# A Fourier filter and a SwiGLU layer on one core: filter read in four large calls, x calls first, dummy matmuls, and norms and stage A placed anew

## The chip, the cores and the metric

The kernel runs on one core of a Trainium2 chip. Five engines work side by side: TensorE (PE in the profile; PEld are its weight loads), VectorE (DVE), ScalarE (ACT), GpSimd (POOL) and SyncE (SP). Each runs its own instructions in the order in which they were issued, and engines wait for each other by semaphores. SP and POOL also issue the DMAs, each from a queue of its own. The metric is device time in microseconds; lower is better.

## What is computed

```python
def _attn_ref(x, filt_r, filt_i):        # x (8, 3008, 256); filters (1505, 256)
    X = np.fft.rfft(x, axis=1)
    Y = X * (filt_r + 1j * filt_i)[None, :, :]
    return np.fft.irfft(Y, n=x.shape[1], axis=1)

def _moe_ref(x, w_gate, w_val, w_out, rms_g):   # w_gate, w_val (256, 1536); w_out (1536, 256)
    xn = x / np.sqrt(np.mean(x * x, axis=-1, keepdims=True) + 1e-06) * rms_g
    g = xn @ w_gate
    return g * (1.0 / (1.0 + np.exp(-g))) * (xn @ w_val) @ w_out
```

The second takes the 24064 rows that the first gives. Everything is float32 outside; inside the matmul operands are float16.

## The kernel before

The transform over 3008 = 47 x 64 points is done as two short transforms, each a matmul with a constant table. For a batch b the stages are:

- A (`a_unit`, 12 units): x times `wa`, written to `t1` (two buffers), stored to DRAM by `z_store`, and read back transposed by `t2_load`. Batch 0 skips DRAM: `a0_unit` and transposes on TensorE (`tr0_unit`).
- B (`b_unit`, 16 units): `t2` times `wb` into a bank psb. Two products with the filter `ff` follow (`s_part` 0 and 1 on VectorE), their sum (`add_unit`, on GpSimd) and a transpose by DMA (`yt_load`). Batch 0 has `yt0_unit` in place of the last two: eight matmuls that add and transpose, and a copy on ScalarE. `b_soft` is the same unit with both products on GpSimd.
- back (`bi_unit`, 16 units): `yt` times `wi` into a bank psi, copied to `uu` by ScalarE, and transposed to `t4` by four DMAs (`t4_load`).
- norms (six a batch, m = 0 to 5): `n_unit` or, for the first two of batch 0, `n_first`; squares on ScalarE, the root on GpSimd (`stat_unit`, `rho`), the scaling on GpSimd (`xt_unit`), a DMA transpose to `xn` (`tr_unit`). Norms 0 and 1 of batch 0 use `q_unit`, `scale_split` and `scale_apply` on TensorE and VectorE.
- the layer: an item (b, m, jt) is one of 12 slices of the hidden width for 512 rows (384 in a few norms). `gv` makes pg and pv (four matmuls), ScalarE makes sg from pg, VectorE makes hh from pv and sg; `down`, two items later, adds four matmuls into po. There are 576 items.

TensorE's accumulator has few banks: psG and psV (pg, pv, two buffers each), psO (two), psM (one) and psB (one). Before the change psM serves `a_unit`, `bi_unit` and `n_unit` in turn, each holding it from its matmul to the end of its copy; psB serves `b_unit`.

The program has a start (lines 550 to 629), in which batch 0 goes through all stages up to its second norm, and a main loop over the items. Around each item a plan puts units of later batches. `at(slot, fn, ...)` enters a unit into the item numbered slot; `fit` moves it on until the bank ("M" is psM, "B" psB) is free in that slot and the estimated load of ScalarE ("A") or VectorE ("V") fits. What is planned first gets its slot first: norm 2 of batch 0, then for each further batch its stage A, its stage B with the back units, and its norms. Norms 3 to 5 of batch 0 are planned after stages A and B of batch 1.

In the start, lines 553 to 576 issue the loads. POOL's queue issues three chunks of x, the filter in calls over 24, 16, 7 and 24 partitions (`f_load`, 26 calls for four tiles, with the fourth x chunk among them), then the weights (`w_load`, 3 x 3 calls). A DMA from POOL's queue waits for the landing of the one eight places before it. The filter tiles are cleared first (`f_zero`), since some rows stay empty. `f_unit` transposes four rows of a tile on TensorE and copies a whole bank into `ff`; the rows of the second half of the frequencies are read in falling order by the DMA:

```python
            for a, e in ((0, 16), (16, 23)):
                nc.gpsimd.dma_start(t[p0 + H + a:p0 + H + e, lo:KC, :],
                                    raw(src, 64 * (a + 1) - c * KC - lo,
                                        [[64 * D, e - a], [-D, KC - lo], [1, D]]))
```

Lines 600 to 618 are a loop of twenty steps: step i does `b_unit` i, `yt0_unit` i - 2 and `bi_unit` i - 4, and in steps 1, 5 and 9 also four `f_unit`s, a `w_load` and a `w_gain` (weights times gain, on GpSimd). Lines 619 to 629 follow: `t4_first` (a transpose of the first four columns of `uu` on TensorE), `t4_load`, `n_first(0)`, `q_unit`, `scale_split`, `scale_apply`, the last `w_gain`, `n_first(1)`, and the x calls of batch 1.

Of the kernel before, what the change touches and what calls it, by code (L numbers as in the profile page):

```python
# [99 lines left out]
def kernel(  # L100
# [101 lines left out]
    def a_unit(b, i, eng="A"):  # L202
        c, r = divmod(i, XC // 2)
        if r == 0:
            st[b]["t1"][c] = t1p.tile([P, XC, D], FP16, tag="t1", name="t1")
        ps = bank(0, "psa")
        nc.tensor.matmul(ps, wa, st[b]["x"][c][:, 2 * r:2 * r + 2, :], start=True, stop=True)  # L207
        copy(eng, st[b]["t1"][c][:, 2 * r:2 * r + 2, :], ps.rearrange("p (a d) -> p a d", a=2))
# [36 lines left out]
    def b_soft(b, i):  # L245
        g, dh = divmod(i, 2)
        ps = bank(3, "psb")[:, 0:4 * KR]
        for k in range(4):
            kk = 4 * g + k
            nc.tensor.matmul(ps[:, ts(k, KR)], st[b]["t2"][kk // KC][:, kk % KC, ds(dh * P, P)],  # L250
                             wb[:, kk, :], start=True, stop=True)
        v = y_tile().rearrange("p a e -> p (a e)")[:, 0:4 * KR]
        nc.scalar.activation(out=v, in_=ps, func=AXT.Copy)
        s = [sp.tile([P, 4, KR], FP16, tag="s%d" % e, name="s%d" % e) for e in range(2)]
        v = v.rearrange("p (k r q) -> p k r q", k=4, r=2)
        st[b]["s"][i] = (v, s)
        s_part(b, i, 0, nc.gpsimd)
        s_part(b, i, 1, nc.gpsimd)
        add_unit(b, i)
# [13 lines left out]

    def bi_unit(b, i, eng="A", bk=0):
        g, dh = divmod(i, 2)
        yt = st[b]["yt"][g]
        ps = bank(bk, "psi")[:, 0:4 * KR].rearrange("p (k j) -> p k j", k=4)
        for k in range(4):
            nc.tensor.matmul(ps[:, k, :], yt[0:KR, k, dh, :], wi[:, 4 * g + k, :], start=True, stop=True)  # L279
        dst = uu[:, :, dh, 16 * g:16 * g + 16].rearrange("p c (k m) -> p c k m", k=4)  # L280
        copy(eng, dst, ps.rearrange("p k (c m) -> p c k m", c=H))
        if i == K2 // 2 - 1:
            half = uu[:, H - 1, :, :].rearrange("p e (k m) -> p e k m", k=K2)
            if b % 2:
                nc.gpsimd.tensor_copy(out=half[:, :, :, 2:4], in_=left)
            else:
                nc.gpsimd.tensor_copy(out=left, in_=half[:, :, :, 0:2])
# [67 lines left out]
    def tr0_unit(g, eng):  # L355
# [5 lines left out]
        if r == 0:  # L361
            t2_tile(0, c)
# [4 lines left out]
    def f_zero(c, eng):  # L367
        t = stg.tile([KR, KC, D], FP32, tag="stg", name="fs")
        if eng == "A":
            nc.scalar.activation(out=t.rearrange("p a d -> p (a d)"),  # L370
                                 in_=mhalf[0:KR, 0:1].to_broadcast([KR, KC * D]), func=AXT.Copy, scale=0.0)
        else:
            nc.vector.memset(t, 0.0)
        fst[c] = t

    def f_load(c):
        t = fst[c]
        lo = 1 if c == 0 else 0
        for src, p0 in ((filt_i, 0), (filt_r, SL)):
            nc.gpsimd.dma_start(t[p0:p0 + H, :, :].rearrange("p a d -> p (a d)"),  # L380
                                raw(src, c * KC, [[64 * D, H], [1, KC * D]]))
            for a, e in ((0, 16), (16, 23)):
                nc.gpsimd.dma_start(t[p0 + H + a:p0 + H + e, lo:KC, :],
                                    raw(src, 64 * (a + 1) - c * KC - lo,
                                        [[64 * D, e - a], [-D, KC - lo], [1, D]]))
            if c == 0:
                nc.gpsimd.dma_start(t[p0 + H:p0 + SL, 0, :], raw(src, 32, [[64 * D, H], [1, D]]))

    def f_unit(c, j, eng, bk):
        half, dh = divmod(j, 2)  # L390
        ps = bank(bk, "psf")[:, 0:4 * KR].rearrange("p (a q) -> p a q", a=4)
        for a in range(4):
            nc.tensor.transpose(ps[:, a, :], fst[c][:, 4 * half + a, ds(dh * P, P)], idf)  # L393
        k0 = KC * c + 4 * half
        copy(eng, ff[:, dh, k0:k0 + 4, SL:3 * SL], ps)

    def f_neg(c):
        k = slice(KC * c, KC * c + KC)
        nc.gpsimd.tensor_scalar(out=ff[:, :, k, 0:SL], in0=ff[:, :, k, SL:2 * SL], scalar1=-1.0,
                                scalar2=1.0, op0=ALU.mult, op1=ALU.mult)  # L400

    def yt0_unit(i, eng, bk):
# [6 lines left out]
        if dh == 0:  # L409
            yt_tile(0, g)  # L410
        copy(eng, st[0]["yt"][g][0:KR, :, dh, :], ps)

    def t4_first():
# [5 lines left out]
        for q, eng in ((0, "A"), (2, "V")):  # L419
# [3 lines left out]
    def n_first(m):  # L423
        y = y_tile()
        sq = xtp.tile([P, 4, D], FP16, tag="xt", name="sq").rearrange("p (a e) d -> p a (e d)", a=2)
        for dh in range(2):
            ps = bank(1 + dh if m == 0 else 0, "psn")
            for q in range(4):
                n1p = 4 * m + q
                src = st[0]["t4f"][:, q] if m == 0 else st[0]["t4"][n1p // XC][:, n1p % XC]  # L430
                nc.tensor.matmul(ps[:, ts(q, P)], src[:, ds(dh * P, P)], wai, start=True, stop=True)
            nc.scalar.activation(out=sq[:, dh, :], in_=ps, func=AXT.Square)
            if m == 0:
                nc.vector.tensor_scalar(out=y[:, dh, :], in0=ps, scalar1=1.0, scalar2=None,
                                        op0=ALU.mult)
            else:
                nc.scalar.activation(out=y[:, dh, :], in_=ps, func=AXT.Copy)
# [3 lines left out]
    def q_unit(m):  # L441
        sq = st[0]["sq"].pop(m)
        ps = psB.tile([P, 4], FP32, tag="mb", name="psq")
        for q in range(4):
            for dh in range(2):
                nc.tensor.matmul(ps[:, q:q + 1], sq[:, dh, ts(q, P)], ones,
# [15 lines left out]
    def scale_apply(m, bk):  # L462
# [8 lines left out]
        for dh in range(2):  # L471
            nc.vector.tensor_tensor(out=xn[:, :, dh, :], in0=ps.rearrange("p (q t) -> p q t", q=4),
                                    in1=y[:, dh, :].rearrange("p (q t) -> p q t", q=4), op=ALU.mult)
# [57 lines left out]
    def w_load(q):  # L531
# [4 lines left out]
        wst[q] = t  # L536
        nc.gpsimd.dma_start(wo[:, ts(q, JT // 3), :],
# [11 lines left out]
    with tc.manual_schedule():  # L549
# [3 lines left out]
        for c in range(3):  # L553
            x_load(0, c)
# [10 lines left out]
        f_zero(0, "V")  # L565
        f_zero(1, "A")
        f_zero(2, "V")
        f_zero(3, "A")
        nc.vector.memset(ones, 1.0)
        f_load(0)  # L570
        x_load(0, 3)
        f_load(1)
        f_load(2)

        E = ("A", "V")
        for dh in range(2):
            a0_unit(0, dh, E[dh], 1 + dh)
        for g in range(4):
            wi_group(g, E[g % 2])
        for gq in (1, 2):  # L580
            for dh in range(2):
                a0_unit(gq, dh, E[dh], 1 + dh)
        for g in range(4, 8):
            wi_group(g, E[g % 2])
        for dh in range(2):
            a0_unit(3, dh, E[dh], 1 + dh)
        for j in range(4):
            f_unit(0, j, E[j % 2], 1 + j % 2)
        f_neg(0)
        f_load(3)  # L590
        for i in range(3):
            for t in ss3[i:i + 1]:
                nc.gpsimd.memset(t, 0.0)
        for gq in (4, 5):
            for dh in range(2):
                a0_unit(gq, dh, E[dh], 1 + dh)
        tr0_unit(0, "V")
        tr0_unit(1, "A")
        UN = K2 // 2
        for i in range(UN + 4):  # L600
            if i < UN:
                b_unit(0, i, (0, 3)[i % 2])
                s_part(0, i, 1)
            if i < 3:
                for g in (2 * i + 2, 2 * i + 3):
                    tr0_unit(g, E[g % 2])
            if i >= 2 and i - 2 < UN:
                yt0_unit(i - 2, "A", 1)
            if i >= 4:
                bi_unit(0, i - 4, "A", 2)  # L610
            if i % 4 == 1 and i // 4 + 1 < NC:
                c = i // 4 + 1
                for j in range(4):
                    f_unit(c, j, E[j % 2], 1 + j % 2)
                f_neg(c)
                w_load(c - 1)
                if c > 1:
                    w_gain(c - 2)
        t4_first()
        for c in range(NXC):  # L620
            t4_load(0, c)
        n_first(0)
        q_unit(0)
        scale_split(0)
        scale_apply(0, 1)
        w_gain(2)
        n_first(1)
        for c in range(NXC):
            x_load(1, c)
# [17 lines left out]
        def fit(slot, *need):  # L647
# [13 lines left out]
            for r, d, cost in need:  # L661
                load[r][slot + d] += cost
# [11 lines left out]
        def a_plan(b, slots, engs):  # L674
            for i in range(12):
                e = engs[i % len(engs)]
                s = fit(slots[i], ("M", 0, 1), (e, 0, 0.6))
                at(s, a_unit, b, i, e)
# [25 lines left out]
        at(1, q_unit, 1)  # L704
        at(3, scale_split, 1)
        at(5, scale_apply, 1, 3)
        norm_plan(0, 2, (12, 14), (2, 3, 6))
        for b in range(1, B):
            t = (b - 1) * 72
            if b == 1:  # L710
                z = a_plan(b, [i for i in range(12)], "AV")
                b_at, lags = [z + 7 + (5 * i + 2) // 3 for i in range(16)], (7, 7)
                soft = range(1, 16, 3)
            elif b == 2:
                z = a_plan(b, [46 + i for i in range(12)], "V")
                b_at, lags, soft = [z + 7 + 5 * i // 2 for i in range(16)], (8, 9), ()
            else:
                at_ = [t - 87 + 4 * i for i in range(12)]
                z = a_plan(b, [s - (s % JT == 1) for s in at_], "V")
# [3 lines left out]
            if b == 1:  # L723
                for m in range(3, 6):
                    norm_plan(0, m, (12 * m - 14, 12 * m - 12), (2, 3, 6))
# [52 lines left out]
```

## Time and profile before

Three runs took 919.36, 917.9 and 919.18 us, with a median of 919.18. The profiled execution took 918.45 us, of which its span, from the first instruction to the last, is 916.7.

| stretch, us | what runs | PE busy | DVE | ACT | POOL | PE clock | DMA GB/s |
|---|---|---|---|---|---|---|---|
| 0 to 20 | tables, x, stage A of batch 0 | 7.04 | 8.58 | 9.34 | 10.64 | see text | 167 |
| 20 to 51 | filter, stages B and back of batch 0 | 29.53 | 23.08 | 23.11 | 24.86 | see text | 193 |
| 51 to 60 | first norm | 4.00 | 3.70 | 3.01 | 4.76 | 0.61 | 167 |
| 60 to 76 | first items | 13.20 | 5.91 | 6.35 | 3.61 | 0.68 | 155 |
| 76 to 160 | items with batch 1 beside them | 81.50 | 55.43 | 55.74 | 38.37 | 1.00 | 120 |
| 160 to 176 | items 59 to 66 | 10.95 | 7.78 | 6.27 | 4.18 | 0.89 | 201 |
| 176 to 916 | the rest | 724.32 | 496.79 | 482.51 | 225.61 | 1.00 | 109 |

Busy times are in us within the stretch. The clock is the share of full speed that TensorE was granted. Up to 29 us the page gives 1.00, but the matmuls show half: eight of L350 take 1.05 us at 17.8 us, and sixteen transposes of L359 take 1.88 us at 27.4 us against 1.06 at 32.0.

How to read the lines. A wait reads "engine, group, <-, who ended the wait: us in total, times, longest us". A line of the timeline reads "start, us, engine, line, operation, written <- read, shape, times", and in brackets the idle time before it and what ended it. Matmuls are pipelined and their ends are modelled, so the distance from one start to the next is the surer measure: two matmuls of 512 columns start 0.22 us apart at full clock.

### The profile page before, as it was taken

The numbers are of one execution on the slowest core, as the hardware profiler recorded it, in microseconds if no ns is written. First come the engines' busy times: TensorE is split into PE (matmuls) and PEld (weight loads), VectorE is DVE, ScalarE is ACT, GpSimd is POOL, SyncE is SP. The second block draws the span as 40 slices with busy tenths as digits, with TensorE's granted clock in tenths as the row PEclk, the third lists the DMA queues.
The fourth block names the chain that finished last, engine by engine and source line by source line (L and its number), as shares of the span: only waits on it lengthen the run. The fifth ranks groups of instructions, "written<-read, shape, count | busy, mean of one in ns | idle before, by whom it ended". The sixth has DMA issues, their size and how long they took to land.

```text
span 916.7 us, 17045 instructions
## 1 busy us (share of the span) xinstructions
PE 870.5 (95%) x6151; PEld 538.3 (59%) x6151; DVE 601.3 (66%) x988; ACT 586.3 (64%) x1264; POOL 312.0 (34%) x362
## 2 busy tenths in 40 slices
PE   4969999799999999999999999999999999999997
PEld 3935555455565556655665566665566666665554
DVE  4836666577767776776767776677666666555554
ACT  4745676467557665677567675677657775677543
POOL 5841572245314441344304442244304441122100
PEclk9969999999999999999999999999999999999999
DMA  9897655896776456665584747543365332431101
GB/s 163 184 195 143 149 88 102 188 186 138 138 145 117 97 116 141 111 146 126 102 178 102 111 104 151 118 122 93 97 131 121 70 70 79 93 75 47 58 24 47
DMA packets 199429, 106.94 MB, mean 117 GB/s; under 512 B 160106, under 2 KB 184168, under 8 KB 199152
## 3 DMA queue, kind: packets, MB, share of 16 engines
q1 hardware_dynamic: 190800, 86.25, 42.2%
q0 software_dynamic: 8544, 19.60, 13.0%
q8 instruction: 48, 0.79, 0.4%
q14 instruction: 37, 0.30, 0.1%
HBM read 44.74 MB, written 35.65 MB: 88 GB/s over the span
## 4 chain that ended last, share of the span: by engine, by line
PE 75%; DVE 9%; ACT 6%; DMA 4%; issue 3%; POOL 2%; SPq 0%; ACTq 0%; DVEq 0%; POOLq 0%
PE po L503 22%; PE pg L486 22%; PE pv L486 20%; DVE hh L491 4%; ACT sg L490 4%; DVE t L198 3%; PE psi L279 3%; PE psb L239 2%; PE psn L307 2%; PE psa L207 2%; DMA wb<-wb_t 1%; DMA xn<-xt 1%; DMA yt<-ss 1%; ACT junk L315 1%; PE psf L393 1%
## 5 line engine op out<-in xcount | busy, mean ns | idle before, releaser
L491 DVE TENSOR_TENSOR hh<-pv,sg 128x512 f16<-128x512 f32 (+1 forms) x576 | 391.6, 680 | 283.7 <-ACT sg L490 192.5
L490 ACT ACTIVATE sg<-pg 128x512 f16<-128x512 f32 (+1 forms) x576 | 337.5, 586 | 265.6 <-PE pg L486 261.2
L503 PE MATMUL po<-wo,hh 128*128 128x256 f16 x2256 | 343.1, 273 | 1.1 <-DVE o L509 0.7
L486 PE MATMUL pg<-xn,wg 128*128 128x512 f16 (+1 forms) x1152 | 339.5, 376 | 4.8 <-DMA xn<-xt 4.8
L486 PE MATMUL pv<-xn,wv 128*128 128x512 f16 (+1 forms) x1152 | 339.4, 376 | 0.0
L503 PEld LDWEIGHTS <-hh 128*128 128x128 f16 x2256 | 212.2, 98 | 119.1 <-issue 11.5
L264 POOL TENSOR_TENSOR ss<-s,s 128x384 f16<-128x384 f16 x112 | 101.8, 910 | 284.5 <-DVE s L232 253.5
L486 PEld LDWEIGHTS <-wv 128*128 128x128 f16 x1152 | 113.3, 98 | 132.1 <-issue 2.3
L486 PEld LDWEIGHTS <-wg 128*128 128x128 f16 x1152 | 112.7, 98 | 19.2 <-issue 6.0
L333 POOL TENSOR_TENSOR xt<-y,rho 128x1024 f16<-128x1024 f32 (+1 forms) x46 | 85.3, 1854 | 2.9
L315 ACT ACTIVATE junk<-y 128x256 f16<-128x256 f32 x180 | 74.2, 412 | 2.8
L196 ACT ACTIVATE uu<-psi 128x384 f16<-128x384 f32 x128 | 62.2, 487 | 12.9 <-PE psi L279 12.4
L229 DVE TENSOR_TENSOR s<-psb,ff 128x384 f16<-128x384 f32 x123 | 67.3, 547 | 2.8 <-PE psb L239 2.6
L232 DVE TENSOR_TENSOR s<-psb,ff 128x384 f16<-128x384 f32 x123 | 67.2, 547 | 0.0
L196 ACT ACTIVATE y<-psn 128x512 f32<-128x512 f32 x92 | 54.1, 588 | 8.7 <-PE psn L307 4.8
L279 PEld LDWEIGHTS <-yt 96*128 96x128 f16 x512 | 35.2, 97 | 40.1 <-issue 14.8
L198 DVE CAST t<-psa 128x512 f16<-128x512 f32 x78 | 53.0, 680 | 0.0
L279 PE MATMUL psi<-wi,yt 96*128 96x96 f16 x512 | 42.8, 205 | 8.9 <-DVE t L198 5.9
L323 POOL TENSOR_SCALAR u<-ss 128x4 f32<-128x4 f32 (+1 forms) x46 | 8.9, 193 | 114.4 <-ACT junk L315 114.0
L325 POOL TENSOR_TENSOR rho<-u,mhalf 128x4 f32<-128x4 f32 (+1 forms) x46 | 46.5, 1010 | 3.8
L239 PE MATMUL psb<-wb,t 96*128 96x96 f16 x492 | 41.4, 207 | 0.3
L239 PEld LDWEIGHTS <-t 96*128 96x128 f16 x492 | 29.4, 98 | 15.1 <-issue 4.7
(82 smaller groups left out, 386.4 us busy)
## 6 DMA issues: line engine op xcount, KB each, us to landing
out_dram<-o SPq DMA_DIRECT2D x40, 512.0 KB, 3.5
xc<-in_x_dram POOLq DMA_DIRECT2D x31, 384.0 KB, 5.8
z_tmp<-t SPq DMA_DIRECT2D x28, 384.0 KB, 4.8
t<-z_tmp SPq DMA_DIRECT2D x28, 384.0 KB, 5.6
out_dram<-o SPq DMA_DIRECT2D x8, 384.0 KB, 3.2
ws<-in_moe_w_gate_dram POOLq DMA_DIRECT2D x3, 512.0 KB, 5.5
ws<-in_moe_w_val_dram POOLq DMA_DIRECT2D x3, 512.0 KB, 6.2
yt<-ss SPq DMA_TRANSPOSE x56, 3.2
```

Of the source, the lines that this page charges most:

```text
L196: nc.scalar.activation(out=out, in_=in_, func=AXT.Copy, **({} if scale is None else {"scale": scale}))
L198: nc.vector.tensor_copy(out=out, in_=in_)
L229: eng.tensor_tensor(out=o, in0=ps, in1=f1, op=ALU.mult)
L239: nc.tensor.matmul(ps[:, ts(k, KR)], st[b]["t2"][kk // KC][:, kk % KC, ds(dh * P, P)], wb[:, kk, :], start=True, stop=True)
L264: nc.gpsimd.tensor_tensor(out=ss3[g % 3][:, :, dh, 0:KR], in0=s[0], in1=s[1], op=ALU.add)
L279: nc.tensor.matmul(ps[:, k, :], yt[0:KR, k, dh, :], wi[:, 4 * g + k, :], start=True, stop=True)
L315: nc.scalar.activation(out=junk, in_=y[:, i, ts(u, D)], func=AXT.Square, accum_out=ss[:, 2 * i + u:2 * i + u + 1])
L333: nc.gpsimd.tensor_tensor(out=xt[:, 0:n, :], in0=y.rearrange("p a (u d) -> p (a u) d", u=2)[:, 0:n, :], in1=rho[:, 0:n].unsqueeze(2).to_br ...
L486: nc.tensor.matmul(ps[:, 0:w], wt[:, dt_, ts(jt, P)], xn[:, 0:nq(b, m), dt_, :], start=(dt_ == 0), stop=(dt_ == 1))
L490: nc.scalar.activation(out=sg[:, 0:w], in_=pg[:, 0:w], func=AXT.Silu)
L491: nc.vector.tensor_tensor(out=hh[:, 0:w], in0=pv[:, 0:w], in1=sg[:, 0:w], op=ALU.mult)
L503: nc.tensor.matmul(po[s4 // 2][:, s4 % 2, :], hh[:, ts(s4, P)], wo[:, jt, :], start=(jt == 0 and s4 % 2 == 0), stop=(jt == JT - 1 and (s4 ...
```

## The change

The start. All four x chunks of batch 0 are issued first. `f_load` makes one call for 94 rows of a filter and half of its columns (four calls in all, 770 KB each, and two calls of one row); nothing has to be cleared but one column of `ff`. `f_unit` transposes four rows of 94 and writes each bank in two copies, one by VectorE and one by ScalarE, with the falling order in the copy's access pattern. All `tr0_unit`s and the `f_unit`s of the first half stand ahead of the twenty-step loop, and the groups are taken in the order 0, 4, 1, 2, 3, 5, 6, 7. Two units (steps 4 and 5) are done by `b_soft` and a DMA transpose. The weights' calls come earlier; `w_gain` and the x calls of batch 1 stand after the second soft unit. The first norm's halves are split by rows instead of by columns. `fill(n)` issues n matmuls of 512 columns on zeros, whose result nobody reads. `n_first(1)` moves into item 2.

The plan. Norms 2 to 5 of batch 0 are planned first, at items 10, 20, 31 and 42. A unit of stage A may take psM or psB and ScalarE or VectorE, whichever fits earliest; with VectorE it keeps its bank for two items.

```diff
-    def a_unit(b, i, eng="A"):
+    def a_unit(b, i, eng="A", bk=0):
...
-        ps = bank(0, "psa")
+        ps = bank(bk, "psa")
...
+    def f_load(f, half):
+        t = stg.tile([P, KC, D], FP32, tag="stg", name="fs")
+        src = (filt_i, filt_r)[f]
+        if half == 0:
+            nc.gpsimd.dma_start(t[0:94].rearrange("p (h a) d -> p h (a d)", h=2),
+                                raw(src, 0, [[16 * D, 94], [12 * D, 2], [1, 4 * D]]))
+            nc.gpsimd.dma_start(t[94:95, 0, :], raw(src, NF - 1, [[D, 1], [1, D]]))
         else:
+            nc.gpsimd.dma_start(t[0:94].rearrange("p a d -> p (a d)"),
+                                raw(src, 4, [[16 * D, 94], [1, KC * D]]))
+        fst[(f, half)] = t
...
+    def f_unit(f, half, j, bk):
+        h, dh = divmod(j, 2)
+        r0 = (12 * h, 4 + 4 * h)[half]
...
+            nc.tensor.transpose(ps[:, a, 0:n], t[0:n, 4 * h + a, ds(dh * P, P)], idf[0:n, 0:n])
+        v = ps.rearrange("p a (q s) -> p s a q", s=4)
...
+        e = ("A", "V") if j % 2 else ("V", "A")
+        copy(e[0], fk[:, :, r0:r0 + 4, o:o + H], v[:, 0:2])
+        hi = slice(o + H, o + 2 * H - 1)
+        if r0:
+            copy(e[1], fk[:, ::-1, 13 - r0:17 - r0, hi][:, :, ::-1, :], v[:, 2:4, :, 0:H - 1])
...
+    def fill(n):
+        ps = psO.tile([P, 512], FP32, tag="po1", name="pf")
+        for _ in range(n):
+            nc.tensor.matmul(ps, wa, ss3[0].rearrange("p k e q -> p (k e q)")[:, 0:512], start=True, stop=True)
...
-        for c in range(3):
+        for c in range(NXC):
             x_load(0, c)
...
+        a0(3, 4, 5)
+        fill(4)
+        for f in range(2):
+            for j in range(4):
+                tr0_unit(ORD[4 * f + j], E[j % 2])
+                f_unit(f, 0, j, 1 + j % 2)
...
+                if p in soft:
...
+                    b_soft(0, unit(p), v)
+                    if p == soft[1]:
+                        yt_load(0, ORD[p // 2])
+                        w_gain(0)
+                        for c in range(NXC):
+                            x_load(1, c)
+                        w_gain(1)
+                        w_gain(2)
...
         t4_first()
+        fill(2)
...
         n_first(0)
+        fill(4)
         q_unit(0)
         scale_split(0)
+        fill(7)
         scale_apply(0, 1)
-        w_gain(2)
-        n_first(1)
-        for c in range(NXC):
-            x_load(1, c)
+        fill(5)
...
+                opts = []
+                for k in "MB":
+                    opts.append((k, "A", ((k, 0, 1), ("A", 0, 0.6))))
+                    opts.append((k, "V", ((k, 0, 1), (k, 1, 1), ("V", 0, 0.68))))
+                k, e, need = min(opts, key=lambda o: fit(slots[i], *o[2], keep=False))
+                s = fit(slots[i], *need)
+                at(s, a_unit, b, i, e, 0 if k == 'M' else 3)
...
-        norm_plan(0, 2, (12, 14), (2, 3, 6))
+        for m, n_at in ((2, 10), (3, 20), (4, 31), (5, 42)):
+            norm_plan(0, m, (n_at, n_at + 2), (2, 3, 6))
...
-            if b == 1:
-                for m in range(3, 6):
-                    norm_plan(0, m, (12 * m - 14, 12 * m - 12), (2, 3, 6))
```

## The prediction

> **What bounds the kernel now.** I read the page first, for the busy shares:
>
> ```profile
> span 916.7 us, 17045 instructions
> PE 870.5 (95%) x6151; PEld 538.3 (59%) x6151; DVE 601.3 (66%) x988; ACT 586.3 (64%) x1264; POOL 312.0 (34%) x362
> PEclk9969999999999999999999999999999999999999
> ```
>
> TensorE sets the time, so time can be won only where it is idle, slow, or held between two matmuls. The third line shows where it is slow: the third slice (46 to 69 us). Second, the waits of TensorE from 60 us on:
>
> ```profile
> PE psi L279 <- DVE t L198: 5.9, 22, 0.6
> PE pg L486 <- DMA xn<-xt: 4.8, 2, 4.5
> PE psa L207 <- DMA xc<-in_x_dram: 2.5, 1, 2.5
> PE psa L207 <- DVE t L198: 1.8, 4, 0.8
> PE psn L307 <- DVE t L198: 0.9, 3, 0.5
> ```
>
> Third, the timeline of TensorE around the two long waits and around one of the many short ones:
>
> ```profile
> 60.23 1.06 PE L486 MATMUL pg<-xn,wg 128*128 128x512 f16 x2
> 61.09 1.06 PE L486 MATMUL pv<-xn,wv 128*128 128x512 f16 x2
> 64.61 0.59 PE L207 MATMUL psa<-xc,wa 128*128 128x512 f16 x1 [2.46 <-DMA xc<-in_x_dram]
> ...
> 160.72 0.60 PE L503 MATMUL po<-wo,hh 128*128 128x256 f16 x4
> 165.81 0.80 PE L486 MATMUL pg<-xn,wg 128*128 128x384 f16 x2 [4.48 <-DMA xn<-xt]
> ...
> 393.01 0.49 PE L486 MATMUL pv<-xn,wv 128*128 128x384 f16 x2
> 394.08 0.33 PE L279 MATMUL psi<-wi,yt 96*128 96x96 f16 x4 [0.59 <-DVE t L198]
> ```
>
> The first block: the loop starts at 60.23 with matmuls of 0.43 us start to start instead of 0.22, and then stands until x of batch 1 lands. The second: item 60 (batch 0, norm 5) has no `xn` for 4.5 us, and its first matmuls run slowly again. The third: psi starts 1.07 us after pv, where two matmuls of that width need 0.33. Its bank psM was filled by `a_unit` one item earlier and VectorE empties it late, because its queue holds hh first.
>
> **The change, part by part.** Times are set against the profiled execution: 918.45 us, of which 916.7 is span; the median of the runs is 0.7 us higher.
>
> *Start, up to the first b_unit (27.10 now).* POOL's queue shows its loads going out as earlier ones land: the waits on x end at 6.47, 8.93 and 11.70 us, so an x chunk takes 2.5 to 2.8 us, and the fourth, now issued at 13.84 behind eight filter calls, is then in by 14.3. a0 for groups 3 to 5 can follow the last wi group at once (17.8 us, about 2.7 us at the slow clock, as 0.86 to 1.05 us each now), and four dummies at 0.43 us end at 22.4. Then comes a stage that the kernel did not have: all eight `tr0_unit` and eight `f_unit` before the first b_unit. ScalarE carries four casts of 1.02 us, eight copies of some 190 elements (rows: 490 ns for 384, 597 for 512, so about 0.33 each) and about 0.7 us of small copies: 7.4 us. The two copies of one bank run one after the other on two engines, which I put at another 1.1. The first b_unit starts near 30.9, 3.8 later than now.
>
> In return the twenty-step loop that follows, which VectorE paces (s_part to s_part 0.47 us, two a unit, 0.93 a step), loses three transposes' casts (2.0 us), swaps six filter copies of 0.55 for eight of 0.36 (0.4), and two units (four s_parts, 1.9) go to POOL: 4.3 us. POOL takes 1.0 + 1.0 + 0.91 us for each, so 5.8 us after the fifth unit's bank is read, and then the transpose's 3.2 us to landing; bi of these units comes eight steps later, 7.4 us. That is 1.6 us short: a wait of 1.5 (0 if the queue slips, 4 if the transfer lands like the slowest ones). The clearing of the filter tiles (two memsets of 1.77 on VectorE, 3.7 us on ScalarE) goes away at no gain, since both engines wait for x at 6.9 us. So far: +3.8 - 4.3 + 1.5 = +1.0.
>
> *Landing of the filter.* Now the eight units of the first half need 1.54 MB, where the first four needed 0.77 (in at 19.98). The trace has no load over 94 partitions. Bounds: at the 410 GB/s of the best stretch (38 to 40 us, wide weight loads) both calls are in by 18.1 and nothing waits. At the 143 GB/s of the filter stage (25 to 30 us), they are in by 14.3 + 10.8 = 25.1 when served in order, +2.7 after 22.4; if all four calls share that rate side by side, by 35.9, +13.5. I take the middle, +2.7, since it is the same tensor on the same queue and the filter loads land there in the order of issue; I keep 0 and +13.5.
>
> The Trainium skill speaks against this part (DMA: Bandwidth & Descriptors, "Why a DMA increments its semaphore by 16 and not by 1"): a transfer is split over the largest number up to 16 that divides its outer dimension, so 94 rows would use two of the 16 engines, where 24 rows use twelve. With that page's 27 GiB/s an engine, 770 KB would take an estimated 13.3 us, in by 27.6, which would make this term +5.2 and the forecast 2.5 us later. The page names an exception for loads from this queue, and no row here shows which holds.
>
> *From the last bi to the first item (50.76 to 60.23).* The chain of waits runs through transposes, t4f, psn, sq, y, u, rho, hl, psr, xn. Its operations stay; the eight psn matmuls of norm 1 (two times about 0.43) leave, psr and psn run at full clock (psr 0.93 to about 0.5), and xn no longer precedes a slow queue: -1.3. The fills (2, 4, 7, 5 of 0.22) lie inside waits of 0.9 to 1.9 us; if that cover went, the longest would cost 1.5. POOL now does three w_gain (2.7 us each) and four x calls (2.5 us) before rho, some 16 us after the first soft unit with its sums; by my times it ends about 1 us before rho is due. At the early end that is free, at the late end +2.
>
> *Items 0 to 12.* From 60.23 to the 14th pg at 87.50 are 27.3 us; thirteen items of 1.30, twelve psa of 0.22 and 0.7 of the first norms make 20.2. So 7.1 are lost to the x wait, the slow clock and psM. x now goes out some 13 us before the loop. New: `n_first(1)` stands inside item 2 with one bank for both halves; its second half waits for sg, sq and y on ScalarE, 1.3 us, and down(0) is queued behind it. Also `z_store` of chunk 0 leaves in item 5 and `a_unit` 6 wants its buffer in item 7: two items of about 1.6 us against 5.4 to landing; the copy waits on ScalarE, sg is queued behind it, and so again for chunk 1. Part is absorbed by two banks of pg: 2.5 us, with 0 and 4 as ends. With 0.4 for the rest: -7.1 + 1.3 + 2.5 + 0.4 = -2.9.
>
> *Item 60.* Norms 3 to 5 of batch 0 go ahead of batch 1; the transpose for item 60 leaves in slot 50 instead of 57. That takes away 4.66 us idle and about 1.7 from the slow clock that followed (165.8 to 169.1). What is late next: batch 1's first transpose now leaves in slot 69 for item 72, three items or 4.2 us ahead, where transposes land in 2.8 to 10.5 us, 3.5 at the median. I put 1.5 (0 to 4). -6.4 + 1.5 = -4.9.
>
> *Stage A elsewhere.* By start-to-start times, 44 places from 176 us on have a VectorE cast of stage A in psM followed in the next item by another user of psM; together they lose 14.6 us (0.33 each). The waits count 8.6, because a modelled matmul's end covers part. After the change such a unit is on ScalarE, or in psB, or keeps its bank for two items. ScalarE copies already in psM followed in the next item (n_unit after bi_unit, 41 places) lose 0.0. ScalarE gains about 55 copies of 0.6 us, 33 us at 65% busy; I give back 2. -12.6.
>
> Sum: 1.0 + 2.7 - 1.3 - 2.9 - 4.9 - 12.6 = -18.0: 900.5 in the profiled execution's terms, 901 as a median.
>
> **The rivals.** (a) The filter calls share their rate side by side: +13.5 instead of +2.7, 912. For it: in the filter stage packets of many calls are under way together. Against it: calls landed in order. (b) ScalarE takes the place of VectorE: its extra copies delay sg, and of the 12.6 us only 3 remain, 910. For it: it is 64% busy on average, and slots such as 50 to 60 hold eight copies. Against: 217 us of its idle time after 200 us is waiting for pg. (c) The fills do not hold the clock, and the change doesn't do that part of what it says: the first items lose another 4 us, 905. (d) Slower: a call over 94 rows lands at the speed of one call now, 192 KB in 7.4 us, or 26 GB/s; 770 KB then take 29.6 us, and the two calls of the first half one after the other end at 73.5. tr0 and f_unit start 51 us late: 949. This decides as soon as the first-half calls land after 22.4 + 2.7 + 18.0 = 43 us; side by side at that speed (43.9) it would just be even.
>
> **How the numbers follow.** The forecast has 0.60 (its own range 892 to 907), (a) 0.15, (b) 0.13, (c) 0.05, (d) 0.07. Low end: no filter wait, no wait for soft units or buffers, and nothing given back on ScalarE take off 10.7: 890. High end: (a), 912. About 0.2% (1.8 us) is what these runs can tell from no change. Faster 0.92, same 0.02, slower 0.06.
>
> **What would show it.** Right: first pg near 62 with matmuls 0.22 apart, no wait of pg for xn around item 60, no psi waiting for DVE t, and f_unit waiting for the filter until about 25 us. Wrong: f_unit starting after 35 us (a, d); sg's waits for pg shrinking while psi or psn wait for ScalarE (b); PEclk low in the third slice (c); or a wait of pg for xn at item 72 over 4 us.

## The result, and the profile after

Twenty runs of the changed kernel have a median of 925.51 us (919.1 to 929.03), twenty of the kernel before 919.11 (916.17 to 920.62). The ratio is 1.0061, with an interval of 1.0045 to 1.0078: slower by about 0.6%, where the forecast was 2% faster. The profiled execution of the changed kernel took 919.34 us, the third fastest of its twenty, so the two profiles lie only 0.9 us apart, and the medians 6.4.

From the page of the changed kernel:

```profile
span 917.6 us, 17059 instructions
PE 864.5 (94%) x6157; PEld 538.9 (59%) x6157; DVE 567.5 (62%) x946; ACT 612.9 (67%) x1326; POOL 305.8 (33%) x345
PEclk9689999989999999999999999999999999999999
```

TensorE has less to do than before (864.5 us instead of 870.5) and still ends later, so it waits more. Its waits over the whole span that bear on the argument (what waits, for whom; us in total, times, longest). Left out are 6.3 us for the first x chunk, 6.2 before, and 3.0 for the table `wb`, 5.6 before:

```profile
PE psf L391 <- DMA fs<-in_filt_i_dram: 15.9, 1, 15.9
PE psa L207 <- DVE t L198: 4.9, 1, 4.9
PE psi L283 <- ACT yt L196: 2.8, 4, 0.7
PE psn L312 <- ACT t L196: 1.8, 1, 1.8
PE pg L499 <- DMA xn<-xt: 1.0, 1, 1.0
```

Of the waits shown before, psi for VectorE's `t` (5.9 us, 22 times) is gone, and pg for xn is down from 4.8 to 1.0 us. Two large ones are new: 15.9 us for the filter and 4.9 us for a tile of stage A. The timeline of TensorE shows the first (start, busy, line, and in brackets the idle time before and its releaser):

```profile
17.57 0.71 PE L364 MATMUL pst<-ident,uu 128*96 128x128 f16 x8
34.17 0.86 PE L391 MATMUL psf<-idf,fs 95*128 95x95 f32 x4 [15.90 <-DMA fs<-in_filt_i_dram]
```

The start times of pg split the span. In us, from the traces of the profiled executions, those of the experiments beside them:

| kernel | up to item 0 | items 0 to 13 | 13 to 62 | 62 to 74 | 74 to the end | span |
|---|---|---|---|---|---|---|
| before | 60.2 | 27.3 | 82.5 | 17.2 | 729.5 | 916.7 |
| after | 77.9 | 23.2 | 76.7 | 23.8 | 716.0 | 917.6 |
| e1_flat_rows | 63.0 | 22.9 | 76.6 | 25.2 | 716.2 | 903.9 |
| e2_eighty_rows | 61.8 | 23.1 | 78.2 | 26.1 | 716.0 | 905.2 |
| e4_batch3_later | 65.4 | 23.2 | 78.2 | 30.2 | 717.0 | 914.0 |
| e6_stageA_alone | 60.8 | 25.4 | 88.7 | 19.0 | 715.5 | 909.4 |
| e7_x3_later | 64.9 | 22.9 | 75.6 | 25.6 | 722.1 | 911.1 |
| e8_A2_spread | 60.6 | 22.7 | 76.9 | 20.6 | 715.7 | 896.5 |
| e9_x3_spaced | 62.8 | 22.5 | 74.8 | 20.0 | 721.6 | 901.7 |
| e10_spread_no_fills | 62.3 | 24.9 | 76.3 | 19.6 | 715.4 | 898.5 |

The changed kernel loses 17.7 us before the first item and 6.6 between items 62 and 74, and wins 4.1, 5.8 and 13.5 elsewhere: +0.9. The experiments take these one by one. Their times are medians; a ratio compares them with runs of the kernel before on the same chip. One execution of e5, at a lower clock than its others, is in the slower state and is left out of its numbers.

A row of the table is one execution, and not always a typical one. Those of e1 and e8 were the fastest of their runs, those of e4, e6 and e7 the slowest, 2.5 to 4.5 us from their medians; a difference of that size between two rows can be the execution's.

### The profile page after: what moved, and what is told of

It is laid out like the page before. It is cut to its first block, busy times and chain, and to the rows that moved or that the text cites. A ratio compares the mean times of both kernels' runs of the same rounds, so it can differ in the third digit from the quotient of the medians.

```text
span 917.6 us, 17059 instructions
## 1 busy us (share of the span) xinstructions
PE 864.5 (94%) x6157; PEld 538.9 (59%) x6157; DVE 567.5 (62%) x946; ACT 612.9 (67%) x1326; POOL 305.8 (33%) x345
## 4 chain that ended last, share of the span: by engine, by line
PE 83%; DMA 7%; DVE 4%; ACT 3%; issue 2%; POOL 1%; SPq 0%; ACTq 0%; DVEq 0%; POOLq 0%
PE po L516 25%; PE pg L499 24%; PE pv L499 24%; DMA fs<-in_filt_i_dram 3%; DMA z_tmp<-t 2%; PE psi L283 2%; PE psb L239 2%; PE psn L312 2%; PE psa L207 2%; ACT sg L503 1%; DVE hh L504 1%; DVE o L522 1%; DMA xn<-xt 1%; PE psy L416 1%; DMA t<-z_tmp 1%
## 5 line engine op out<-in xcount | busy, mean ns | idle before, releaser
L266 POOL TENSOR_TENSOR ss<-s,s 128x384 f16<-128x384 f16 x114 | 103.7, 910 | 267.7 <-DVE s L232 246.3
L229 DVE TENSOR_TENSOR s<-psb,ff 128x384 f16<-128x384 f32 x121 | 66.2, 547 | 5.7 <-PE psb L239 3.9
L232 DVE TENSOR_TENSOR s<-psb,ff 128x384 f16<-128x384 f32 x121 | 66.2, 547 | 0.0
L196 ACT ACTIVATE t<-psa 128x512 f16<-128x512 f32 x61 | 35.9, 596 | 6.3 <-DMA z_tmp<-t 2.4
## 6 DMA issues: line engine op xcount, KB each, us to landing
fs<-in_filt_i_dram POOLq DMA_DIRECT2D x2, 752.0 KB, 29.4
```

Source lines behind the costliest of these rows:

```text
L196: nc.scalar.activation(out=out, in_=in_, func=AXT.Copy, **({} if scale is None else {"scale": scale}))
L229: eng.tensor_tensor(out=o, in0=ps, in1=f1, op=ALU.mult)
L232: eng.tensor_tensor(out=o, in0=ps[:, :, ::-1, :], in1=f2, op=ALU.mult)
L266: nc.gpsimd.tensor_tensor(out=ss3[g % 3][:, :, dh, 0:KR], in0=s[0], in1=s[1], op=ALU.add)
```

## The experiments

### Where the 15.9 us for the filter come from

The DMA view of the changed kernel over 0 to 45 us gives, in 40 equal slices, the busy share of the 16 engines in tenths and the rate, then an issue with its median time to landing:

```profile
DMA  0197999999999999999933222222222310000079
GB/s 0 33 70 134 201 221 244 243 248 242 236 232 79 193 187 227 222 204 157 149 69 98 95 102 106 102 106 106 98 85 106 131 80 36 0 0 0 4 138 419
fs<-in_filt_i_dram POOLq DMA_DIRECT2D x2, 752.0 KB, 29.4
```

From 23 to 33 us only two to three tenths of the engines are busy, and the rate is 100 GB/s. The packets tell which call this is: all are pieces of 4 KB, those of the first half, on 4.1 engines, 25 GB/s each; the 8 KB pieces of the second half, issued later, had run on some 12 engines before. Of the 16 increments by which the first call reports its landing, 14 came at 15 to 16 us and the last two at 33.1 and 33.7 us: two engines carried it. Of the two calls of the second half, twelve increments each had come by 22.1 and 25.7 us, and the last four at 35.5 to 38.6: on four engines they stood behind the first half's rows. e1 writes the same bytes in two dimensions instead of three:

```diff
-            nc.gpsimd.dma_start(t[0:94].rearrange("p (h a) d -> p h (a d)", h=2),
-                                raw(src, 0, [[16 * D, 94], [12 * D, 2], [1, 4 * D]]))
+            for h in range(2):
+                nc.gpsimd.dma_start(t[0:94, 4 * h:4 * h + 4].rearrange("p a d -> p (a d)"),
+                                    raw(src, 12 * h, [[16 * D, 94], [1, 4 * D]]))
```

> Edit: the changed kernel, but each first-half filter call (94 rows x two pieces of 4 KB, three dimensions) is written as two calls of 94 rows x one piece of 4 KB (two dimensions, as the second-half calls have). Same bytes, same pieces, same queue, two calls more. Theory A (few engines: a call of the three-dimensional form is given to 2 of the 16 DMA engines, at about 25.7 GB/s each, which the trace of the changed kernel shows as 103 GB/s on 4 engines from 25 to 33 us): the first half is spread over 16 engines and lands at 20 to 23 us, the first f_unit starts by 24 us instead of 34.2, the first pg at 65 to 68 us instead of 77.9, and the run takes 905 to 911 us. The spread of the changed kernel's runs (919 to 929 us) should shrink to that of the kernel before (4 us) if it comes from this landing. Rival B (the calls share one rate, whatever their form): f_unit still starts at 33 to 35 us, and the time stays at 919 to 929 us. Rival C (the landing moves but the loop behind it is held by something else, such as the soft units' transposes): f_unit by 24 us, first pg not before 72 us, 913 us or more.

910.13 us (905.62 to 913.31), ratio 0.9907, interval 0.9886 to 0.9927: 15.4 us below the changed kernel's median, at the upper end of what theory A gave. The same view of e1, and a line of its timeline:

```profile
DMA  0187999999999999999996002999990006999999
fs<-in_filt_i_dram POOLq DMA_DIRECT2D x2, 376.0 KB, 12.1
```

```profile
20.54 0.50 PE L392 MATMUL psf<-idf,fs 95*128 95x95 f32 x4
```

All engines are busy until the filter is in, its first half lands in 12 to 13 us, and f_unit starts at 20.5 us with no idle time before it. B and C are out: the calls share no fixed rate, since the bytes moved at 240 to 280 GB/s in e1 and at 100 in the changed kernel while twelve engines stood idle, and the first pg moved by 14.9 us, with the landing. What did not shrink as expected is the spread of the runs (7.7 us). e2 keeps the three dimensions and changes the number of rows alone:

```diff
+            for lo, n in ((0, 80), (80, 14)):
+                nc.gpsimd.dma_start(t[lo:lo + n].rearrange("p (h a) d -> p h (a d)", h=2),
+                                    raw(src, 16 * lo, [[16 * D, n], [12 * D, 2], [1, 4 * D]]))
```

> Edit: the changed kernel; each first-half filter call of 94 rows is cut into one of 80 rows and one of 14, in the same three-dimensional form (two pieces of 4 KB a row). Theory A (the form is spread over the largest number up to 16 that divides its rows: 2 for 94, 16 for 80, 14 for 14): the first f_unit starts at 20 to 22 us as with the flat rows, 904 to 913 us. Rival (three dimensions alone put a call on two engines, whatever its rows): f_unit at 33 to 36 us, 918 to 930 us.

One run, 906.95 us. From its DMA view and TensorE's timeline:

```profile
fs<-in_filt_i_dram POOLq DMA_DIRECT2D x1, 640.0 KB, 13.6
fs<-in_filt_i_dram POOLq DMA_DIRECT2D x1, 112.0 KB, 13.3
```

```profile
18.45 0.50 PE L392 MATMUL psf<-idf,fs 95*128 95x95 f32 x4
```

80 and 14 rows of the slow form land nearly as fast as the flat one: it is the number 94, in this form, that puts a call on two engines. The Trainium skill ("DMA: Bandwidth & Descriptors", section "Why a DMA increments its semaphore by 16 and not by 1") gives this rule, and the runs agree with it: largest divisor up to 16, so 2 for 94. They fit its exception too, for some direct copies from this queue, which are dealt out over 16 engines, the share of each rounded up: the two-dimensional calls of 94 rows behaved so (15 engines busy in e1), the three-dimensional ones not.

### Where the 13.5 us of stage A come from

e6 puts only the changed planner of stage A into the kernel before:

```diff
-                e = engs[i % len(engs)]
-                s = fit(slots[i], ("M", 0, 1), (e, 0, 0.6))
-                at(s, a_unit, b, i, e)
+                opts = []
+                for k in "MB":
+                    opts.append((k, "A", ((k, 0, 1), ("A", 0, 0.6))))
+                    opts.append((k, "V", ((k, 0, 1), (k, 1, 1), ("V", 0, 0.68))))
...
+                at(s, a_unit, b, i, e, 0 if k == 'M' else 3)
```

> Edit: the kernel before, with only the changed planner of stage A (each unit takes the first free slot over psM or psB and ScalarE or VectorE, a VectorE copy keeps its bank for two slots); start, filter, norms and item order of the kernel before. Theory A (stage A's VectorE copies in psM cost the 12.6 us of the forecast): from item 74 to the end the run takes 715 to 719 us as in the changed kernel, instead of 729.5; batch 3's first unit moves from slot 69 to 60 here too, which brings the same wait of about 5 us before item 74; in all 909 to 915 us. Rival B (the 13.5 us came from the norms' new places, or from psi and psn being less crowded): item 74 to the end still takes 727 us or more, and the run 918 us or more. Rival C (ScalarE's extra copies give back most of it): 723 to 727 us in that stretch.

908.7 us, ratio 0.9893, interval 0.9877 to 0.9908. From item 74 to the end it takes 715.5 us, as the changed kernel does: theory A (its total is 0.3 us below the range). Rivals B and C are out. Its waits from 190 us on have no psi for `t` left; but between 86 and 195 us there is a new one, of the same kind as the changed kernel's at 178 us, and longer:

```profile
PE psa L207 <- ACT t L196: 9.1, 1, 9.1
PE pg L486 <- DMA xn<-xt: 2.1, 1, 2.1
```

It is not the one that was expected, of batch 3's first unit. It stands in item 58, and the tile is batch 2's own: ScalarE's copy waits for the store of that batch's second chunk, which was issued at 161.4, behind three transposes (ScalarE's timeline):

```profile
166.62 0.60 ACT L196 ACTIVATE t<-psa 128x512 f16<-128x512 f32 x1 [9.54 <-DMA z_tmp<-t]
```

So the planner that wins the 13.5 us also makes such waits: with two banks and two engines to choose from, it packs batch 2's twelve units into slots 50 to 59 (47 to 59 in e6), where the old one took 48 to 67.

### What is late between items 62 and 74

In the changed kernel, VectorE's and SP's timelines around the wait of 4.9 us:

```profile
182.85 0.69 DVE L198 CAST t<-psa 128x512 f16<-128x512 f32 x1 [6.04 <-DMA z_tmp<-t]
```

```profile
175.83 0.56 SPq L212 DMA_DIRECT2D z_tmp<-t  x1
176.44 7.01 SPq L297 DMA_TRANSPOSE t<-uu  x2
183.56 0.51 SPq L212 DMA_DIRECT2D z_tmp<-t  x1
```

Batch 3's first unit stands in slot 60 and needs a `t1` buffer whose store left at 175.8 and landed seven microseconds later. e4 is e1 with that unit six slots later:

```diff
-                at_ = [t - 87 + 4 * i for i in range(12)]
+                at_ = [66 + 7 * i // 2 if b == 3 else t - 87 + 4 * i for i in range(12)]
```

> Edit: the kernel of the flat rows, and stage A of batch 3 planned from slot 66 on (66 + 7i/2) instead of slot 57 on (57 + 4i), so that its first unit lands in slot 66 instead of 60, with nothing else changed. Theory (the 4.9 us wait of psa at 178 us in the changed kernel is the t1 tile of batch 3 waiting for the z_store of batch 2's chunk 2, which the transposes on SP's queue hold up): the wait goes, items 62 to 74 take 17 to 19 us instead of 23.8, and the run is 4 to 7 us faster than the kernel of the flat rows. Rival (SP's queue is what is late, and the next thing on it takes the wait: pg for xn at item 72, or psb for t2): items 62 to 74 still take 22 us or more, or 74 to 86 grow by as much, and the time is within 1.5 us of the flat rows.

912.63 us, ratio 0.9924, interval 0.9896 to 0.9952: no gain over e1. The theory fell: the wait of psa is gone, but, as the rival had it, the next thing on SP's queue took its place (only the time, 2.5 us above e1, is a little outside the rival's 1.5). In the profiled execution items 62 to 74 took 30.2 us (SP's timeline, then TensorE's):

```profile
162.27 17.41 SPq L297 DMA_TRANSPOSE t<-uu  x2
```

```profile
187.51 0.50 PE L239 MATMUL psb<-wb,t 96*128 96x96 f16 x4 [14.30 <-DMA t<-z_tmp]
```

Two transposes held SP for 17.4 us, one of them for 13.5. In e1, whose plan is the same up to slot 60, that transpose took 3.6: the crowd makes it late by very different amounts from run to run. The packets of that time show x chunks of batch 3 (3 KB pieces from GpSimd's queue) on 4 to 15 engines, from 171 us on a store of batch 2 beside them (3 KB pieces too, from SP's queue), and the transposes' 256-byte reads at 13 to 71 GB/s until 178 us; when both were in, these rose to 182. So the packets of e4 do not tell x loads from stores. e7 moves the x loads:

```diff
-                        at(s + 2, x_load, b + 1, i // 3)
+                        at(max(s + 2, 63 + 2 * (i // 3)) if b == 2 else s + 2, x_load, b + 1, i // 3)
```

> Edit: the kernel of the flat rows; the x loads of batch 3 leave in slots 63, 65, 67 and 69 instead of 53, 56, 59 and 61, and stage A of batch 3 is planned from slot 74 on (74 + 8i/3), since it needs them. Batch 2's stage A, its stores and the transposes of batch 1 stay in slots 50 to 60. Theory A (what is late around item 60 are the transposes of batch 1 on SP's queue, and they are late because x of batch 3, on GpSimd's queue, is fetched in the same microseconds: with 3 KB packets on 6 to 15 engines one transpose took 13.5 us in the run with batch 3 later): the four transposes take 1.3 to 3.5 us each, items 62 to 74 take 17 to 19 us instead of 25.2, the median is 6 to 9 us below the 910 of the flat rows, and the runs lie within 5 us of each other. Rival B (the stores of batch 2's stage A, bunched in the same slots, do it): transposes stay at 3 us or more in the sum of two 6 to 17 us, items 62 to 74 take 22 us or more, time within 2 us of the flat rows. Rival C (the x loads collide with the next thing, the transpose for item 72, in slots 63 to 69): pg waits 4 us or more for xn at item 72.

910.04 us, ratio 0.9899, interval 0.9881 to 0.9917: nothing gained. Rival C came in a form of its own. Batch 1's last two transposes took 6.0 us (7.1 in e1), and the one for item 72 now met the x loads and took 9.8, with a wait of TensorE behind it (SP's timeline, then the waits from 140 to 220 us):

```profile
172.38 9.75 SPq L347 DMA_TRANSPOSE xn<-xt  x1
```

```profile
PE psb L239 <- DMA t<-z_tmp: 8.3, 1, 8.3
```

Items 86 to 146 also took 97.2 us instead of 91.3, with new waits for t4 and t2 of 1.7 and 1.5 us. e8 thins out the crowd instead, with two edits at once:

```diff
-                z = a_plan(b, [46 + i for i in range(12)])
+                z = a_plan(b, [46 + 7 * i // 4 for i in range(12)])
...
+                at_ = [69 + 3 * i if b == 3 else t - 87 + 4 * i for i in range(12)]
```

> Edit: the kernel of the flat rows; stage A of batch 2 is planned over slots 46 + 7i/4 instead of 46 + i, and that of batch 3 from slot 69 on (69 + 3i), so that the stores of batch 2, the x loads of batch 3 and the transposes of batch 1 share slots 52 to 67 as in the kernel before, instead of 52 to 61. Theory A (too much is sent at once around slots 52 to 61): items 62 to 74 take 17 to 20 us instead of 25.2, and the run is 5 to 9 us faster than with the flat rows. Under theory A with the x loads alone to blame, two x loads still stand beside the transposes, so it should gain less than the kernel with x of batch 3 later; with the stores to blame, more. Rival (batch 2 then is late itself): psb waits for t2 or items 74 to 146 take more than 111 us.

900.87 us (898.32 to 901.93), ratio 0.9805, interval 0.9789 to 0.9822: 9.3 us below e1 and faster than both kernels of the case. Items 62 to 74 took 20.6 us. Both are just outside the ranges of theory A (5 to 9 faster, 17 to 20). The rival is out: items 74 to 146 took 110.1 us, below its 111. The four transposes now hold SP for 9.4 us in all (5.8 and 7.1 in e1), no unit waits for a `t1` buffer there, and two waits of TensorE are left there (SP's timeline, then the waits from 140 to 220 us):

```profile
152.25 9.40 SPq L297 DMA_TRANSPOSE t<-uu  x4
```

```profile
PE pg L500 <- DMA xn<-xt: 3.6, 1, 3.6
PE psn L312 <- DMA t<-uu: 1.2, 1, 1.2
```

Of the 7.4 us between the two spans, 4.6 lie in items 62 to 74 and 2.4 ahead of item 0, which the edit doesn't touch. e9 went after the 3.6 us:

```diff
-                        at(s + 2, x_load, b + 1, i // 3)
+                        at(s + 2 if b != 2 or i == 2 else 67 + i, x_load, b + 1, i // 3)
```

> Edit: the kernel with batch 2's stage A spread; of batch 3's x loads only the first keeps its slot (53), the other three leave in slots 72, 75 and 78 instead of 56, 62 and 67. Batch 3's stage A needs them from slots 80, 92 and 107. Theory A (x loads on GpSimd's queue beside the transposes on SP's queue are what makes the transposes late; in the kernel before this one 4.2 us for one of batch 1's four and 3.6 us of waiting of pg for xn at item 72): batch 1's four transposes take 1.3 to 2.5 us each, no wait of pg for xn over 1 us at item 72, items 62 to 74 take 17 to 18 us instead of 20.6, 3 to 4 us faster. Rival B (the stores and the transposes alone do it): the same as beside it within 1.5 us. Rival C (the three loads now meet the yt transposes of batch 2, from slot 78 on): psi waits for yt, items 74 to 146 take 113 us or more instead of 110, same or slower.

> The kernel with batch 2's stage A spread, once more, so that the two beside it are compared on one chip: 898 to 903 us.

e8 again took 900.77 us (ratio 0.9835, interval 0.9814 to 0.9856), e9 902.95 (0.984, 0.9817 to 0.9864): no gain. From GpSimd's and SP's timelines of e9 and TensorE's waits from 140 to 220 us:

```profile
167.89 0.65 POOL L187 DMA_DIRECT2D xc<-in_x_dram  x1
```

```profile
167.97 1.29 SPq L347 DMA_TRANSPOSE xn<-xt  x1
```

```profile
PE psi L283 <- DMA yt<-ss: 4.8, 1, 4.8
PE pg L500 <- DMA xn<-xt: 4.3, 1, 4.3
```

A slot orders a queue, it does not delay it. GpSimd had nothing to do between slot 66 and slot 72, so the load of slot 72 left at 167.9, together with the transpose it was to avoid; the other two met batch 2's transposes, as rival C had it (items 74 to 146 took 115.9 us). So in each of e4, e7, e8 and e9 a transpose with an x load beside it was late. The packets of e9 show it without a store: from 169 to 172 us the x chunk held up to 16 engines, and the reads of the transpose, issued at 168, moved at most 15 GB/s. But they were slow again from 173 to 174.5 (25 and less), with the chunk in, so the x load is not all of it. Moving just the one load behind work that holds it back was not run, nor was the changed kernel with its slow calls and batch 2 spread; whether the t2 loads behind the transpose share the blame is open.

### The dummy matmuls

e5 is e1 without its 22 dummies, e10 is e8 without them (the lines `fill(n)` removed).

> Edit: the kernel of the flat rows without any of the dummy matmuls (no fill calls at all, 22 matmuls less); nothing else changes. Theory A (the dummies hold the clock at the first items): the granted clock falls to half between the last bi_unit and the first items, the matmuls of the first items run 0.43 us apart as in the kernel before, and the run takes 3 to 6 us more than with the flat rows. Rival (the clock does not fall in so short a chain, or the dummies only take TensorE's time): within 1 us of the flat rows, or up to 2 us faster.

> Edit: the kernel with batch 2's stage A spread, without any of the 22 dummy matmuls. The pair of flat-rows kernels with and without them differed by 3.7 us with intervals of 2 us and more each, in runs that the collision around item 60 scattered. Theory A (the dummies hold the clock): 2 to 5 us more than beside it, the first item starts at 62 to 66 us instead of 60.6 and the first two items run at half clock. Rival (that difference was scatter): within 1 us.

e5 took 913.83 us (906.85 to 917.13; ratio 0.9932, interval 0.991 to 0.9955), 3.7 more than e1; the intervals overlap. e10 took 901.01 (0.9812, 0.979 to 0.9834), which is e8 within 0.3. The first item with and without them, from TensorE's timelines of e8 run again and of e10:

```profile
61.44 0.59 PE L500 MATMUL pg<-xn,wg 128*128 128x512 f16 x2 [0.30 <-DVE xn L485]
62.52 0.59 PE L500 MATMUL pg<-xn,wg 128*128 128x512 f16 x2
```

```profile
62.34 1.01 PE L500 MATMUL pg<-xn,wg 128*128 128x512 f16 x2 [1.47 <-DVE xn L485]
64.43 1.06 PE L500 MATMUL pg<-xn,wg 128*128 128x512 f16 x2
```

The dummies do hold the clock: over these two items TensorE was granted 1.00 of full speed with them and 0.50 without, 1.08 us an item instead of 2.09, some 2 us. That the total shows none of it says only that 2 us lie within what these runs can tell.

## Why the prediction was wrong

Its steps against the two profiled executions, in us ("item 60" is measured over items 13 to 62, "item 72" over 62 to 74):

| step | predicted | measured |
|---|---|---|
| start up to the first b_unit, without the filter wait | +3.8 | +0.3 |
| landing of the filter | +2.7 | +15.9 |
| loop of sixteen units (-4.3 +1.5) | -2.8 | +3.3 |
| from the last bi to the first item | -1.3 | -1.8 |
| items 0 to 13 | -2.9 | -4.1 |
| item 60 | -6.4 | -5.8 |
| item 72 | +1.5 | +6.6 |
| stage A elsewhere | -12.6 | -13.5 |
| sum | -18.0 | +0.9 |

**Landing of the filter** is the step that failed: 13.2 of the 18.9 us between forecast and profile. It took 143 GB/s from the filter stage of the kernel before, "since it is the same tensor on the same queue". The rate was not the tensor's or the queue's: those calls were over 24 and 16 rows, and in that stage 13 of the 16 engines were busy (a share of 0.83) where the two new calls had four. Rival (a) put a price near the measured one (+13.5) on a mechanism, four calls that share 143 GB/s to the end, which e1 shows to be wrong; that the price was near is luck. Rival (d) had the right kind of limit, a call's own, and the wrong size: 26 GB/s a call, where two engines by themselves gave 51. The rule that was quoted against the change was the right one, and its +5.2 was short because both calls also met the second half's, issued behind them: while those ran, from 16 to 23 us, the first half's four engines moved 40 to 53 GB/s in all, afterwards 103.

**The start** was priced 3.5 us too high: the four dummies that were to end at 22.4 us ended near 17.6. With the wider calls, where nothing waits for the filter, the first b_unit came at 26.0 to 28.4 us, against 27.1 before.

**The loop of sixteen units** was expected to gain from VectorE's lighter load. It takes 23.4 us before and 26.7 in the changed kernel, and no less than 26.3 in any kernel with the new start, fast landing or not. Two places in the trace go with it. The second half's f_units stretch steps 2 and 3 to 3.2 and 3.9 us, each bank waiting for two copies on two engines in turn. And psi waits four times 0.7 us for ScalarE's yt: with the two soft units put back to ninth and tenth place, the four units ahead of these move up two steps, and `bi_unit` takes each in the step in which its `yt0_unit` is issued. This is read from the trace and the order of issue; no run undid it, so the cause is argued and not shown. The wait for the soft units' transpose, priced at 1.5, is nothing in the changed kernel's profile. In e4, and likewise in e7, it is there (TensorE's waits of e4, 26 to 68 us):

```profile
PE psi L283 <- DMA yt<-ss: 1.2, 1, 1.2
```

In both the matmuls behind it ran at half rate for some 3 us, and the loop took 29.2 us.

**Item 72** was mis-sized, by 5.1 us, and misplaced: the wait fell on item 62. The transpose's slot was looked at, but not what the new planner does to batch 2: twelve units, four stores, four x loads and four transposes in items 50 to 62.

The rest held: stage A to 0.9 us (e6 gets the same without any other part), which rules out rival (b), item 60, the chain to the first item, and items 0 to 13. In those, the wait for a `t1` buffer that was priced at 2.5 is the 1.8 us of psn for ScalarE's `t`, with a store's landing of 6.9 us behind it, and n_first(1)'s wait, priced at 1.3, measured 1.2. The low end of the range is added up wrongly: the terms named for it (2.7, 1.5, 2.5 and 2) make 8.7, not 10.7, so 892.

What stays open is why the median of the changed kernel lies 6 us above its profiled execution. Two places vary between kernels that are alike there: the crowded slots (items 62 to 74 took 23.8, 25.2 and 26.1 us in three kernels with the same plan) and the loop (26.3 to 26.7 or 29.2 us, with or without the wait for the soft units). They could make 6 us together, but the other runs of the changed kernel have no profile.

## What to carry to other kernels

Price a load by how many DMA engines its form is given, not by the rate of another load of the same tensor: one narrow call also holds up the wide ones behind it. A planner that gets more freedom uses it at the earliest slot; count what then leaves in the same few microseconds on every queue, stores and loads included. And before a load is moved to a later slot, see what on its queue would hold it back.

## What the runs showed that was not expected

- The same first-half bytes landed in 29.4 us on 2 engines a call, and in 12 to 16 in either wider form.
- A DMA transpose on SP's queue took 1.5 us alone and up to 13.5 beside x loads of GpSimd's queue and a store, and held all that SP issues behind it.
- The changed planner of stage A by itself, in the kernel before, gives 908.7 us; the whole change, with its filter calls flat and batch 2's stage A spread, 900.8.
